# K transposed by crossbar DMA in nearly all heads, and K loads issued in two parts: a two-block attention backward pass

## The chip, the cores and the metric

The kernel runs on one core of a Trainium2 chip. The metric is the device time of one execution in microseconds; three runs of the kernel before gave 1694.41, 1717.56 and 1721.23 us, so the median is 1717.56 us. A core has five engines that run beside each other: PE (TensorE: matrix products and transposes), DVE (VectorE), ACT (ScalarE), POOL (GpSimd) and SP (SyncE, which here only issues DMA transfers). The DMA engines, 16 for this core, move the data. All wait for each other through semaphores.

## The reference

Two independent attention blocks, A and B, with inputs of the same shapes. The kernel computes the output of both and the gradients of all ten inputs.

```python
B, Sq, D = 8, 96, 640
H, Sk, Dh = 32, 512, 128
q = (x @ wq).reshape(B, Sq, H, Dh).transpose(0, 2, 1, 3)
scores = jnp.einsum("bhqd,bhkd->bhqk", q, k_cache) * (Dh ** -0.5)
p = _softmax(scores, axis=-1)
o = jnp.einsum("bhqk,bhkd->bhqd", p, v_cache)
return o.transpose(0, 2, 1, 3).reshape(B, Sq, H * Dh) @ wo
...
_out, _vjp = jax.vjp(_f, A_x, A_k_cache, A_v_cache, A_wq, A_wo, B_x, B_k_cache, B_v_cache, B_wq, B_wo)
_grads = _vjp(grad_out)
```

All tensors are bf16. The K and V caches and their gradients are the large ones: 32 heads x 8 batches x 512 x 128 for each block.

## The kernel before, in words

The unit of work is one (head, batch): 2 blocks x 32 heads x 8 batches = 512 of them, called ticks, at about 3.3 us each. One tick goes through a software pipeline of steps that are spread over later ticks:

- S1 (`c_s1`, L280): K of this batch, 128 x 4 x 128, is transposed in four pieces on PE, and DVE copies the result from PSUM to the tile `KT_pe`. Only for batches that `k_on_pe` (L548) names.
- S2 (`c_s2a`, L291, and `c_s2b`, L304): scores = Q K^T, one matmul of 512 columns (L298) that needs the transposed K; DVE takes the row maximum, ACT the exponential.
- S3 (L315, L324): the reciprocal on DVE, the scaling of P on POOL.
- S4, S5 (`c_s45`, `c_s4`): P transposed on PE, output and dV.
- S6 (`c_s6`, L411): dP, which needs V transposed (`VT`), and dS.
- S7, S8: dK, dS transposed, dQ.

Work of a whole head (projections, transposes of Q and dO, weight gradients) is hooked onto certain ticks of the head, so some ticks hold little more than the pipeline and others twice as much.

**K and V.** `c_ld` (L262) loads the K or V of two batches (a pair, `NB = 2`) with one DMA of 256 KB: 128 partitions, 2 x 512 elements in each. K has 7 buffers, V 5. `c_xt` (L272) transposes a whole pair by a crossbar DMA from SBUF to SBUF: `VT` for all pairs, with 4 buffers, and `KT` for those pairs that are not on PE, with 2 buffers. `k_on_pe` sends to PE every even pair, all pairs of head 0 and, in the first block, those of head 1. That makes 268 batches on PE and 122 pairs (244 batches) by DMA.

**Order.** All loads and crossbar transposes are issued by SP, in one stream in program order; stores of dK and dV and the loads of weights are issued by POOL. The Emitter sorts the steps by tick and by slot within a tick. `OFF` (L45) gives the ticks: the K load of a pair at -5, the V load at -3, KT at -3, VT at 0, S2 at +3, S6 at +6, S8 at +8. S2 and S3 are put in with high priority, and a scheduler may place an instruction later than its tick where a buffer is not yet free. A new KT needs its buffer back: the last reader of the KT of two uses earlier is the second S2 of that pair. The semaphores of SP's DMAs are eight in number and are used in turn.

Of the kernel before, what the change touches and what calls it, by code (L numbers as in the profile page):

```python
# [46 lines left out]
EV = dict(pB0="act", pB1="dve", pC00="act", pC01="act", pC10="act", pC11="dve", pD0="dve", pD1="dve", qA0="act", qA1="dve", qB0="act", qB1="dve", qD="dve", gU="act")  # L47
GSPREAD0 = 9
PRIO_OFF = 2000
GSPREAD1 = 9  # L50
SLOTS = dict(LOAD=0, S2A=5, S2B=5.5, S1=6, S8=10, S7=20, S5=30, S4=40, S6=50, S3A=52, S3B=53, S5B=54, HEAD=SL_HEAD, GRP=SL_GRP)


def build_block(tc, em, tick0, blk, x, kc, vc, wq, wo, g_all, out_all, dx, dk, dv, dwq, dwo, ident, ones, pools, HG=6, first=True, groups=None):
    nc = tc.nc
# [7 lines left out]
    KC = Sk // 128  # L63
    NB = 2
# [197 lines left out]
    def c_ld(h, b, n, bufs):  # L262
        def f():
            src = kc if n == "K" else vc
            X = kvp.tile([128, NB, KC, 128], BF16, name=n + "_sb", bufs=bufs)
            nc.sync.dma_start(X[:], src[b:b + NB, h].rearrange("b (p c) d -> p b c d", c=KC))
            for i in range(NB):
                st = CS.setdefault((blk, h, b + i), {})
                st[n + "_sb"], st[n + "_all"] = X[:, i], X
        return f  # L270
# [20 lines left out]
    def c_s2a(h, b):  # L291
        def f():
            with tc.high_priority(PRIO_OFF):
                st = CS[(blk, h, b)]
                hs = HS[(blk, h)]
                tok = slice(b * Sq, (b + 1) * Sq)
                S_ps = bank([Sq, Sk], F32, "S_ps")
                nc.tensor.matmul(S_ps[:], hs["QT_h"][:, tok], st["KT"], start=True, stop=True)  # L298
                negm = wk.tile([Sq, 1], F32, name="negm", bufs=3)
                nc.vector.tensor_reduce(negm[:], S_ps[:], axis=AX.X, op=ALU.max, negate=True)  # L300
                st["S_ps"], st["negm"] = S_ps, negm
        return f

    def c_s2b(h, b):  # L304
        def f():
            with tc.high_priority(PRIO_OFF):
                st = CS[(blk, h, b)]
                E_sb = wk.tile([Sq, Sk], BF16, name="E_sb", bufs=2)
                rowsum = wk.tile([Sq, 1], F32, name="rowsum", bufs=3)
                nc.scalar.activation(E_sb[:], st["S_ps"][:], ACT.Exp, bias=st["negm"][:], scale=1.0, accum_out=rowsum[:])  # L310
                st["E_sb"], st["rowsum"] = E_sb, rowsum
                del st["S_ps"]
        return f

    def c_s3a(h, b):  # L315
        def f():
            with tc.high_priority(PRIO_OFF):
                st = CS[(blk, h, b)]
                rinv = wk.tile([Sq, 1], F32, name="rinv", bufs=3)
                nc.vector.reciprocal(rinv[:], st["rowsum"][:])  # L320
                st["rinv"] = rinv
        return f

    def c_s3b(h, b):  # L324
        def f():
            with tc.high_priority(PRIO_OFF):
                st = CS[(blk, h, b)]
                P_sb = wk.tile([Sq, Sk], BF16, name="P_sb", bufs=5)
                pinned(nc.gpsimd.tensor_scalar(P_sb[:], st["E_sb"][:], st["rinv"][:], 0.0, op0=ALU.mult, op1=ALU.add))  # L329
                st["P_sb"] = P_sb  # L330
# [215 lines left out]
    NTS = len(tsplits)  # L546

    def k_on_pe(h, b):  # L548
        return (b // NB) % 2 == 0 or h == 0 or (first and h == 1)

    SX = pools["SX"]
    for g in range(NG):
        h0 = GH0[g]
        for hh in range(groups[g]):
            h = h0 + hh
# [16 lines left out]
            for b in range(B):  # L572
                ct = c0t + b
                if b % NB == 0:
                    em.add(tick0 - 12 if first and h == 0 and b == 0 else ct + OFF["ldk"], SLOTS["LOAD"], c_ld(h, b, "K", 7))
                    em.add(ct + OFF["ldv"], SLOTS["LOAD"], c_ld(h, b, "V", 5))
                    if not k_on_pe(h, b):
                        em.add(ct + OFF["kt"], SLOTS["LOAD"] + 1, c_xt(h, b, "KT", 2))
                    em.add(ct + OFF["vt"], SLOTS["LOAD"] + 1, c_xt(h, b, "VT", 4))
                if k_on_pe(h, b):  # L580
                    em.add(ct + 2, SLOTS["S1"], c_s1(h, b))
                em.add(ct + OFF["s2"], SLOTS["S2A"], c_s2a(h, b))
                em.add(ct + OFF["s2"], SLOTS["S2B"], c_s2b(h, b))
                em.add(ct + OFF["s3"], SLOTS["S3A"], c_s3a(h, b))
                em.add(ct + OFF["s3"], SLOTS["S3B"], c_s3b(h, b))
                em.add(ct + OFF["s5"], SLOTS["S5B"], c_s5b(h, b))
                if b % 2 == 1:
                    em.add(ct + OFF["s4"] + 1, 54.3, c_st(h, b, "v"))
                    em.add(ct + OFF["s7"] + 1, 54.3, c_st(h, b, "k"))
                em.add(ct + OFF["s4"], SLOTS["S4"], c_s4(h, b))  # L590
                for i, o in enumerate(("s8", "s7", "s5", "s4")):
                    SX.setdefault(ct + OFF[o], [None] * 4)[i] = (blk, h, b)
                em.add(ct + OFF["s6"], SLOTS["S6"], c_s6(h, b))
                em.add(ct + OFF["s7"], SLOTS["S7"], c_s7(h, b))
# [9 lines left out]
        gs0 = max(3, (GSPREAD0 * groups[g]) // HG)  # L604
        gs1 = max(3, (GSPREAD1 * groups[g]) // HG)
        if not first and g == NG - 2:
# [16 lines left out]
def _kernel_impl(tc, A_x, A_k_cache, A_v_cache, A_wq, A_wo, B_x, B_k_cache, B_v_cache, B_wq, B_wo, grad_out,  # L623
           out_0, out_1, out_2, out_3, out_4, out_5, out_6, out_7, out_8, out_9, out_10, HG=6, slots=None, off=None, hk=None, ev=None, gspread=None, groupsA=None, groupsB=(6, 6, 6, 6, 6, 2)):
    global GSPREAD0, GSPREAD1
    nc = tc.nc
# [8 lines left out]
    if gspread:  # L635
        GSPREAD0, GSPREAD1 = gspread
    with ExitStack() as ctx:
# [104 lines left out]
```

## Time and profile before

| what | before |
|---|---|
| runs | 1694.41, 1717.56, 1721.23 us |
| profiled execution | span 1699.8 us (the page gives no other time of it) |
| granted PE clock | 0.998 |
| PE busy | 1675.7 us (99%) |
| K transposes on PE (L285) | x1072 matmuls, 104.0 us busy |
| copies to KT_pe on DVE (L287) | x268, 410 ns median |
| KT by DMA (L275) | x122, 1250 ns median issue on SP |
| VT by DMA (L275) | x256, 1440 ns median issue on SP |
| K loads (L266) | x256, 256 KB, 5.2 us median to landing |
| mean DMA rate | 249 GB/s |

"Busy" is the time in which an engine, or a group of instructions, has at least one in work. Matmuls are pipelined, so that their durations overlap. A line such as `PE S_ps L298 <- DMA KT<-K_sb: 2.1, 1, 2.1` in the view of waits says that PE stood idle ahead of the instruction that writes S_ps at line 298 until the DMA that writes KT had landed: 2.1 us in total, 1 time, 2.1 us at the longest. PEld is the part of PE that loads the stationary operand, and SPq the sequencer of SP. In a timeline, the columns are start, duration, engine, line, operation and tiles. The share of a DMA queue is the sum of its packets' times over 16 engines; packets of different queues overlap, so that the sum can pass 100%.

### The profile page before, as it was taken

The page shows a single profiled execution, that of the slowest core. Times are in us where ns is not written, and L with a number is a line of the kernel's source. Part 1 is how long each engine was busy: PE and PEld are TensorE (multiplying, and loading weights), DVE is VectorE, ACT ScalarE, POOL GpSimd, SP SyncE. Part 2 cuts the span into 40 slices and gives each one's busy share as a digit, 9 for nine tenths or more (in the row PEclk, how much of TensorE's full clock was granted, in tenths as well). Part 3 has the DMA queues.
Part 4 walks back from the last instruction along what each step waited for, and adds up shares of the span by engine and source line. Part 5 has one row for each costly group of instructions (what it writes and reads, how often), then busy time and mean ns, then how long its engine had stood idle before and what let it go on. Part 6 is the DMA issues. An engine that isn't in the chain of part 4 may idle for free.

```text
span 1699.8 us, 56567 instructions
## 1 busy us (share of the span) xinstructions
PE 1675.7 (99%) x22024; PEld 1343.8 (79%) x22024; DVE 1329.8 (78%) x3052; ACT 1405.2 (83%) x3518; POOL 1040.3 (61%) x1747
## 2 busy tenths in 40 slices
PE   8999999999999999999999999999999999999999
PEld 7877778778778778777778877887788778778876
DVE  6887678878788878787778876787788778878877
ACT  6998889869869869878768998897799679878975
POOL 3676567646647647656566764675576557656754
PEclk9999999999999999999999999999999999999999
DMA  9999999999999999999999999999899989999994
GB/s 256 252 259 250 258 225 260 262 242 243 262 221 252 268 238 259 225 251 237 281 256 269 273 270 248 238 289 248 218 261 276 237 221 261 281 217 240 263 247 141
DMA packets 600429, 423.05 MB, mean 249 GB/s; under 512 B 419360, under 2 KB 557984, under 8 KB 600160
## 3 DMA queue, kind: packets, MB, share of 16 engines
q1 hardware_dynamic: 546576, 242.08, 72.2%
q0 software_dynamic: 53584, 177.35, 32.7%
q8 instruction: 173, 2.83, 0.7%
q14 instruction: 96, 0.79, 0.2%
HBM read 161.09 MB, written 159.12 MB: 188 GB/s over the span
## 4 chain that ended last, share of the span: by engine, by line
PE 89%; DMA 4%; ACT 3%; issue 1%; DVE 1%; POOL 0%; SPq 0%; DVEq 0%; ACTq 0%; POOLq 0%
PE q_ps L243 12%; PE o_ps L512 12%; PE dwo_ps L470 6%; PE dV_ps L389 6%; PE dK_ps L432 6%; PE S_ps L298 6%; PE dP_ps L417 6%; PE dwq_ps L490 6%; PE x_ps L340 5%; PE x_ps L365 5%; PE dst_ps L346 5%; PE x_ps L359 5%; PE kT_ps L285 3%; PE n_ps L258 3%; PE nat_ps L455 2%; DMA VT<-V_sb 1%
## 5 line engine op out<-in xcount | busy, mean ns | idle before, releaser
L329 POOL TENSOR_SCALAR P_sb<-E_sb,rinv 96x512 bf16<-96x512 bf16 x512 | 352.6, 689 | 567.8 <-DVE rinv L320 559.2
L310 ACT ACTIVATE E_sb<-S_ps,negm 96x512 bf16<-96x512 f32 x512 | 351.0, 686 | 187.6 <-DVE negm L300 181.9
L421 DVE SCALAR_TENSOR_TENSOR dS_sb<-dP_ps,dl_ps,P_sb 96x512 bf16<-96x512 f32 x512 | 382.1, 746 | 60.9 <-PE dl_ps L419 54.6
L300 DVE TENSOR_REDUCE negm<-S_ps 96x1 f32<-96x512 f32 x512 | 347.6, 679 | 50.9 <-PE S_ps L298 46.6
L435 ACT ACTIVATE dK_sb<-dK_ps 128x512 bf16<-128x512 f32 x512 | 302.1, 590 | 63.4 <-PE dK_ps L432 56.5
L392 ACT ACTIVATE dV_sb<-dV_ps 128x512 bf16<-128x512 f32 x512 | 311.6, 609 | 0.0
L378 ACT ACTIVATE PT_sb<-x_ps 128x384 bf16<-128x384 bf16 x512 | 253.1, 494 | 0.0
L512 PEld LDWEIGHTS <-OD 128*128 128x128 bf16 x1536 | 132.2, 98 | 100.4 <-issue 1.0
L398 POOL DMA_DIRECT2D out_dram<-dV_sb x256 | 194.9, 761 | 11.8 <-issue 8.6
L398 POOL DMA_DIRECT2D out_dram<-dK_sb x256 | 195.0, 762 | 9.1 <-issue 4.4
L389 PE MATMUL dV_ps<-dOnat_h,P_sb 96*128 96x128 bf16 x2048 | 198.2, 219 | 0.8 <-DVE dOnat_h L160 0.6
L417 PE MATMUL dP_ps<-VT,dOT_h 128*96 128x512 bf16 x512 | 195.4, 382 | 3.0 <-DMA VT<-V_sb 3.0
L432 PE MATMUL dK_ps<-Qnat_h,dS_sb 96*128 96x128 bf16 x2048 | 198.1, 219 | 0.1
L407 POOL TENSOR_TENSOR prod<-OD,dOT_h 128x96 bf16<-128x96 bf16 x512 | 184.2, 360 | 13.8 <-ACT OD L375 12.6
L348 DVE COPY dST_sb<-dst_ps 128x384 bf16<-128x384 bf16 x512 | 177.1, 346 | 10.5 <-PE dst_ps L346 10.3
L365 PE MATMUL x_ps<-ident,P_sb 96*128 96x96 bf16 x2048 | 172.0, 205 | 0.8 <-POOL P_sb L329 0.3
L359 PE MATMUL x_ps<-PT_sb,V_sb 128*128 128x96 bf16 x2048 | 172.3, 206 | 0.2 <-ACT PT_sb L378 0.2
L346 PE MATMUL dst_ps<-ident,dS_sb 96*128 96x96 bf16 x2048 | 172.3, 206 | 0.2 <-DVE dS_sb L421 0.2
L340 PE MATMUL x_ps<-dST_sb,K_sb 128*128 128x96 bf16 x2048 | 171.0, 206 | 1.3 <-ACT dK_sb L435 0.8
L375 ACT ACTIVATE OD<-x_ps 128x192 bf16<-128x192 f32 (+1 forms) x515 | 167.9, 326 | 3.9 <-PE x_ps L340 3.9
L320 DVE RECIPROCAL rinv<-rowsum 96x1 f32<-96x1 f32 x512 | 79.9, 156 | 106.0 <-ACT E_sb L310 100.4
L340 PEld LDWEIGHTS <-K_sb 128*128 128x128 bf16 x2048 | 131.1, 98 | 25.1 <-issue 1.6
(84 smaller groups left out, 3744.4 us busy)
## 6 DMA issues: line engine op xcount, KB each, us to landing
out_dram<-dV_sb POOLq DMA_DIRECT2D x256, 256.0 KB, 5.2
out_dram<-dK_sb POOLq DMA_DIRECT2D x256, 256.0 KB, 5.3
K_sb<-in_A_k_cache_dram SPq DMA_DIRECT2D x128, 256.0 KB, 5.3
V_sb<-in_A_v_cache_dram SPq DMA_DIRECT2D x128, 256.0 KB, 5.2
K_sb<-in_B_k_cache_dram SPq DMA_DIRECT2D x128, 256.0 KB, 5.0
V_sb<-in_B_v_cache_dram SPq DMA_DIRECT2D x128, 256.0 KB, 4.9
out_dram<-dwo_sb POOLq DMA_DIRECT2D x63, 160.0 KB, 4.8
out_dram<-dwq_sb POOLq DMA_DIRECT2D x31, 320.0 KB, 6.1
```

The source lines that it names most:

```text
L300: nc.vector.tensor_reduce(negm[:], S_ps[:], axis=AX.X, op=ALU.max, negate=True)
L310: nc.scalar.activation(E_sb[:], st["S_ps"][:], ACT.Exp, bias=st["negm"][:], scale=1.0, accum_out=rowsum[:])
L329: pinned(nc.gpsimd.tensor_scalar(P_sb[:], st["E_sb"][:], st["rinv"][:], 0.0, op0=ALU.mult, op1=ALU.add))
L340: nc.tensor.matmul(dQT_ps, st["K_sb"][:, c, :], st["dST_sb"][:, c * Sq:(c + 1) * Sq], start=(c == 0), stop=(c == KC - 1))
L389: nc.tensor.matmul(dV_ps[:, c * 128:(c + 1) * 128], P_sb[:, c * 128:(c + 1) * 128], hs["dOnat_h"][:, b * 128:(b + 1) * 128], start=True, s ...
L392: nc.scalar.activation(SB[(blk, h, b // 2, "v")][:, b % 2], dV_ps[:], ACT.Identity, scale=1.0)
L398: pinned(nc.gpsimd.dma_start(dst[b - 1:b + 1, h].rearrange("b (p c) d -> p b (c d)", c=KC), SB.pop((blk, h, b // 2, which))[:]))
L417: nc.tensor.matmul(dP_ps[:], hs["dOT_h"][:, tok], st["VT"], start=True, stop=True)
L421: nc.vector.scalar_tensor_tensor(dS_sb[:], dP_ps[:], dl_ps[:, 0:1], st["P_sb"][:], op0=ALU.subtract, op1=ALU.mult)
L432: nc.tensor.matmul(dK_ps[:, c * 128:(c + 1) * 128], dS_sb[:, c * 128:(c + 1) * 128], hs["Qnat_h"][:, b * 128:(b + 1) * 128], start=True, s ...
L435: nc.scalar.activation(SB[(blk, h, b // 2, "k")][:, b % 2], dK_ps[:], ACT.Identity, scale=1.0)
L512: nc.tensor.matmul(o_ps[:], src[:, t * 128:(t + 1) * 128], rhs, start=(hh == 0), stop=(hh == groups[g] - 1))
```

## The change

K of every head but the first (in the first block: but the first two) is transposed by crossbar DMA; and each K load becomes two DMAs on SP, one for partitions 0 to 119 and one for 120 to 127. The data and the arithmetic stay the same. `KT` keeps its 2 buffers, and `OFF` is unchanged.

```diff
+SPLIT_LD = ("K",)
...
             X = kvp.tile([128, NB, KC, 128], BF16, name=n + "_sb", bufs=bufs)
-            nc.sync.dma_start(X[:], src[b:b + NB, h].rearrange("b (p c) d -> p b c d", c=KC))
+            v = src[b:b + NB, h].rearrange("b (p c) d -> p b c d", c=KC)
+            if n in SPLIT_LD:
+                nc.sync.dma_start(X[0:120], v[0:120])
+                nc.sync.dma_start(X[120:128], v[120:128])
+            else:
+                nc.sync.dma_start(X[:], v)
...
     def k_on_pe(h, b):
-        return (b // NB) % 2 == 0 or h == 0 or (first and h == 1)
+        return h == 0 or (first and h == 1)
```

After it, 24 batches are left on PE (8 of head 0 in each block, 8 of head 1 in the first), and 244 pairs go by DMA in place of 122. SP issues 512 K load DMAs in place of 256.

## The prediction

> **What bounds the kernel now.** I read the page from the top: busy shares, the chain that ended last, the DMA queues; then the waits, the tile views of the two crossbar-transposed tiles, and a timeline of one tick.
>
> ```profile
> PE 1675.7 (99%) x22024; PEld 1343.8 (79%) x22024; DVE 1329.8 (78%) x3052; ACT 1405.2 (83%) x3518; POOL 1040.3 (61%) x1747
> ...
> q1 hardware_dynamic: 546576, 242.08, 72.2%
> q0 software_dynamic: 53584, 177.35, 32.7%
> ...
> PE 89%; DMA 4%; ACT 3%; issue 1%; DVE 1%; POOL 0%; SPq 0%; DVEq 0%; ACTq 0%; POOLq 0%
> ```
>
> TensorE (PE) is never idle and holds 89% of the chain; nothing else is near. But the two DMA queues add up to 105% of 16 engines: the transfers are the second limit, and close. They are hidden today, as the waits show:
>
> ```profile
> PE dP_ps L417 <- DMA VT<-V_sb: 3.0, 2, 2.4
> ...
> PEld L298 <- DMA KT<-K_sb: 2.5, 2, 2.3
> ...
> PE S_ps L298 <- DMA KT<-K_sb: 2.1, 1, 2.1
> ```
>
> PE stood still for transposed tiles for under 8 us in the whole run. How long they take from issue to landing (min/median/max, first KT, then VT):
>
> ```profile
> L275 SPq DMA_TRANSPOSE KT<-K_sb x122: 1231/1250/3126, 44.3 to 1647.3; - x122
> ...
> DMA to landing us min/median/max: 3.1/5.2/11.9
> ```
>
> ```profile
> L275 SPq DMA_TRANSPOSE VT<-V_sb x256: 1231/1440/6143, 12.2 to 1656.9; - x128
> ...
> DMA to landing us min/median/max: 3.1/6.1/14.9
> ```
>
> And what four K transposes cost on PE, from one tick:
>
> ```profile
> 807.75 0.39 PE L285 MATMUL kT_ps<-ident,K_sb 128*128 128x128 bf16 x4
> 807.92 0.24 PEld L340 LDWEIGHTS <-K_sb 128*128 128x128 bf16 x4
> 807.97 0.33 PE L340 MATMUL x_ps<-dST_sb,K_sb 128*128 128x96 bf16 x4
> ```
>
> The next group starts 0.22 us after this one: 0.22 us is the price, not the 0.39 us of the row. The 1072 such matmuls end 56 ns apart in the median.
>
> **The change part by part.**
>
> *Removed from PE.* 268 of 512 batches are transposed on PE now; afterwards 24 are (8 of head 0 in each block, 8 of head 1 in the first). 244 x 4 x 56 ns = 55 us, with the slower first ones 56 us. PE is the bound, so this counts in full: 1699.8 - 56 = 1644 us. Row against rule: in this row a matmul lasts 219 ns but ends 56 ns after the last. The Trainium skill, page "Trainium Kernel Development and Optimization", section Performance Expectations, warns that matmul busy time is a bad metric because matmuls are pipelined; agreed. By the busy time of the group (104.0 us for 1072) the gain would be 95 us.
>
> *Removed from DVE.* 244 copies KT_pe x 410 ns = 100 us, off a 78% busy engine. Nothing on the path: PE waited 0.8 us for them. ACT stays at 1405 us, 85% of 1644, and does not become the bound.
>
> *Added to SP and the DMA engines.* 122 KT transposes (122 x 1.40 us mean issue = 171 us of SP) and 256 more load issues (about 0.48 us each, the K_sb load's median: 123 us). SP's loads and transposes take 939 us today, so 1233 of 1644 us afterwards, in order. Per pair (two ticks, 6.4 us) that is five DMAs. Each waits for the one eight places before it, 10 us earlier, where 95% of the VT have landed (10.2 us): a rare wait. V and K loads keep leads of 24 and 35 us, VT one of 18 to 20 us, against landings of 5 to 6: costed at nothing, and only a landing over 15 us would uncover them.
>
> *The wait that is added.* KT has two buffers. Today only odd pairs use them, so a KT is issued some 20 us before its S2. Afterwards every pair does: KT of pair p may be issued only when PE has done the second S2 of pair p-2, three ticks before its own S2. In the built order of the changed kernel this wait stands on every KT. I counted the PE instructions from that release to the first S2 of the pair, each at the pace at which such matmuls end in this trace (56 ns for 128 columns, 43 for 96, about 216 for 512), scaled by 1.036 to the span: 7.0 us in the shortest twentieth, 8.6 median, 10.9 upper quartile (a tick without head work is short). SP takes about 0.4 us of it on average, finishing the VT issued just before. Behind the waiting KT on SP stand the next V and K loads, whose leads bear it; behind the waiting S2 on PE stands all of PE, so a late KT costs its full lateness.
>
> How late? Pairing every such lead with every landing time of today's 122 KT: 5% are late, 0.063 us on average, x 244 = 15 us. With those of the 256 VT: 19%, 0.34 us, x 244 = 82 us. These are my bounds. Today's KT is issued a median 4.2 us behind its VT, afterwards 1.3 us, so it will queue behind it. The nearest rows lie between: 39 transposes issued 2.0 to 2.6 us behind another landed in 6.3 us median, ten under 2.0 us behind in 5.3. I take the middle, 48 us, less 8 us for the split (next): 40 us.
>
> *The split.* In the packet records of this trace the transposes (256-byte packets, 18 ns in the median) freeze 235 times on nearly all engines at once, for 0.96 us in the median, 230 us in all, and all end together; inside, about one packet of that queue is in progress: one engine catches up, and the others stand. In 59% of these an instruction fetch began in the 2 us before (28% at random moments). An engine that moves no K would be spared 256 x 16 packets x 42 ns = 174 us. The skill, "DMA: Bandwidth & Descriptors", section Why a DMA increments its semaphore by 16 and not by 1, says that the engine count is the largest number up to 16 dividing the outer dimension, on the lowest-numbered engines: 15 for 120 partitions, 8 for 8, so the last engine carries no K. The same page's Rules for kernel authors speak against it: two transfers to disjoint partitions are not worth it, one of 128 partitions is better. No row shows either. By the first rule, if the last engine is the laggard, landings shorten: VT's landings cut by a tenth make 47 us of the 82, KT's make 8 of the 15. By the second the split gives nothing. From the rows alone: bounds 0 (another engine lags) and 35 us (that tenth of VT's landings); I take 8, near the lower end, since no row names the laggard.
>
> *Sum.* -56 + 40 = -16 us on 1699.8, i.e. 1684. The page gives the span alone; the three runs are 1694 to 1721, and the median 1717.6 lies 17.8 above the span, which I keep: 1701.6.
>
> **The rivals.**
>
> *The waits stay small.* If the split removes most freezes, landings fall by a tenth (8 us of waits, from KT): -48, 1669 us. For: PE waits under 8 us for transposes now. Against: the lead shrinks from 20 to 8.6 us.
>
> *Slower: KT waits take more than PE gave.* One mechanism: VT and KT back to back on SP, KT landing like VT or later. VT's landings give -56 + 82 = +26, 1744 us; a tenth longer 131 us of waits, +75, 1792 us. For: 32% more transposes on queues already at 105%. Against: a waiting PE lets the DMA drain, and one late KT gives the next more time. It decides from 0.23 us mean wait per KT (no gain), 0.37 us for 2% slower.
>
> *The hardware queue becomes the bound.* q1 has a packet in flight for 1382 us; 122 transposes more, 2.36 us from first to last packet each, make 1670 us, plus the 24 us in which PE idles today: 1694 span, 1712 us. Against: 0.6 us of the 2.36 are freezes, and packets of two transfers overlap.
>
> *The split does nothing:* the forecast without its 8 us, 1709 us; within its range.
>
> **How the numbers follow.** Forecast 0.40 (its own range 1677 to 1744, waits of 15 to 82 us); small waits 0.25; slower 0.27; queue bound 0.08. A measurement here tells about 2% from no change: 1683 and 1752. Faster: 0.25 plus 0.08 of the forecast's low end = 0.33. Slower: 0.25 of the 0.27. Within: 0.42. The range reaches from 1660 (no waits: 1662) to 1785; about 0.06 lie below and 0.12 above.
>
> **What would show it** (line numbers of the changed kernel, six or seven higher). K transposes on PE, L291, x96, and copies KT_pe x24; PE's work shorter by 56 us; waits of PE and PEld at S2, L304, for KT, 15 to 82 us in all; KT landing near 6 us; SP waiting at L281 for S2. Wrong if those waits pass 110 us, if PE waits for VT or V_sb, or if KT waits stay under 10 us and the span is near 1650. The split's step is right if freezes and VT's landing shrink.

## The result and the profile after

| | before | after |
|---|---|---|
| median | 1709.61 us (1694.41 to 1721.23, 4 runs) | 1873.73 us (1855.3 to 1881.82, 4 runs) |
| ratio, 95% interval | | 1.0973 [1.0882, 1.1065] |
| span of the profiled execution | 1699.8 us | 1853.5 us |
| granted PE clock, mean | 0.998 | 0.969 |
| PE idle (worked out from the PE records) | 19 us | 170 us |

The changed kernel is 9.7% slower, and its time lies above the range that was given. (The profiled execution of before took 1701.65 us: its span lies 1.85 us under its own time, so the 17.8 us between span and median that the prediction kept are mostly the spread between executions.)

The page of after: busy shares, the two DMA queues, and the chain that ended last, by engine and by line.

```profile
PE 1677.7 (91%) x21048; PEld 1318.8 (71%) x21048; DVE 1258.3 (68%) x2808; ACT 1407.5 (76%) x3518; POOL 1039.4 (56%) x1747
...
q1 hardware_dynamic: 677200, 274.08, 79.5%
q0 software_dynamic: 53584, 177.35, 30.3%
...
PE 58%; DMA 36%; ACT 3%; issue 1%; DVE 1%; POOL 0%; SPq 0%; DVEq 0%; ACTq 0%; POOLq 0%
DMA KT<-K_sb 35%; PE o_ps L518 11%; PE q_ps L244 6%; PE dwq_ps L496 5%; PE S_ps L304 4%; PE dwo_ps L476 4%; PE dK_ps L438 4%; PE dV_ps L395 4%; PE dP_ps L423 4%; PE dst_ps L352 3%; PE x_ps L371 3%; PE x_ps L346 3%; PE x_ps L365 3%; PE n_ps L259 2%; PE nat_ps L461 1%
```

976 matmuls went (22024 to 21048: 244 x 4), yet PE's busy time did not fall. PE held 89% of the chain before; now it holds 58%, and one transfer, K's transpose, 35%. The view of waits names the same transfer:

```profile
PEld L304 <- DMA KT<-K_sb: 170.1, 93, 5.6
PE S_ps L304 <- DMA KT<-K_sb: 148.6, 82, 5.4
```

Both lines are one stall seen by PE's two halves. No line of this view names VT, V_sb or a K load for PE. Issue times on SP in the tile views of KT and of VT (min/median/max in ns):

```profile
L281 SPq DMA_TRANSPOSE KT<-K_sb x244: 1232/2775/5037, 40.2 to 1811.7; - x122
```

```profile
L281 SPq DMA_TRANSPOSE VT<-V_sb x256: 1231/1392/5444, 14.1 to 1810.3; - x128
```

The median issue of a KT went from 1250 to 2775 ns; that of a VT stayed. The last three columns of the view by windows are granted clock, DMA share and GB/s. First two windows of before, then the same two of after and a short one:

```profile
300.00:600.00 300.00, 299.33 (x3927) 238.91 (x3925) 240.81 (x554) 247.30 (x621) 184.79 (x310) 1.00 1.08 250
900.00:1200.00 300.00, 299.68 (x3996) 241.68 (x3994) 232.82 (x531) 263.20 (x661) 193.09 (x324) 1.00 1.09 260
```

```profile
300.00:600.00 300.00, 274.14 (x3500) 215.11 (x3500) 211.78 (x473) 231.42 (x581) 173.32 (x292) 0.99 1.15 251
900.00:1200.00 300.00, 275.83 (x3442) 216.05 (x3440) 201.76 (x452) 232.22 (x583) 175.01 (x293) 0.96 1.10 253
...
990.00:995.00 5.00, 3.93 (x26) 2.59 (x27) 1.75 (x4) 1.26 (x3) 0.39 (x1) 0.50 1.39 310
```

The DMA engines move as many GB/s as before (251 and 253 against 250 and 260) while there is more to move; the share was 1.08 to 1.09 before and is 1.10 to 1.15 now. One stall: first the last reader of the KT two uses earlier, in the view of L304 for 973 to 978 us, then the timeline of after.

```profile
L304 PE MATMUL S_ps<-KT,QT_h x1: 379/379/379, 975.3 to 975.3; 128*96 128x512 bf16 x1
```

```profile
975.89 0.33 SPq L270 DMA_DIRECT2D K_sb<-in_B_k_cache_dram  x1
976.32 5.44 SPq L281 DMA_TRANSPOSE VT<-V_sb  x1
981.87 3.76 SPq L281 DMA_TRANSPOSE KT<-K_sb  x1
...
984.00 0.34 PE L365 MATMUL x_ps<-PT_sb,V_sb 128*128 128x96 bf16 x4
...
991.07 0.63 PE L304 MATMUL S_ps<-KT,QT_h 128*96 128x512 bf16 x1 [4.82 <-DMA KT<-K_sb]
...
994.26 0.53 PE L365 MATMUL x_ps<-PT_sb,V_sb 128*128 128x96 bf16 x4
```

PE freed the KT buffer at 975.7 us (975.3 and 0.38). SP had the second part of a K load and a VT to issue first, and the VT took it 5.44 us; the KT came only then, 6.2 us after its release, and landed 9.1 us later. PE stood still for 4.8 us. From 989.0 us, still within the stall, its clock is granted at one half for 6.8 us (0.50 in the short window): the same four matmuls of L365 take 0.53 us in place of 0.34.

**The account.** 1699.8 - 56 (K transposes off PE) + 151 (PE idle, 19 to 170 us) + 53 = 1848 us, against a span of 1853.5. The 56 us are the prediction's estimate, by the count of matmuls. The 53 us: within the span the clock was granted at 0.5 in 27 stretches of 3.4 or 6.8 us, 112.6 us in all, which loses 56.3 us; before, two such stretches lost 3.4 us. In the records each of the 27 begins inside a gap in PE's work of 1.8 to 6.5 us or within 8 us after it; ten gaps of that size were followed by none. That explains why PE's busy time did not fall.

### The profile page after: what moved, and what is told of

Same layout as the page of the kernel before. It is cut to its first block, busy times and chain, and to the rows that moved or that the text cites. A ratio compares the mean times of both kernels' runs of the same rounds, so it can differ in the third digit from the quotient of the medians.

```text
span 1853.5 us, 55160 instructions
## 1 busy us (share of the span) xinstructions
PE 1677.7 (91%) x21048; PEld 1318.8 (71%) x21048; DVE 1258.3 (68%) x2808; ACT 1407.5 (76%) x3518; POOL 1039.4 (56%) x1747
## 3 DMA queue, kind: packets, MB, share of 16 engines
HBM read 161.09 MB, written 159.12 MB: 173 GB/s over the span
## 4 chain that ended last, share of the span: by engine, by line
PE 58%; DMA 36%; ACT 3%; issue 1%; DVE 1%; POOL 0%; SPq 0%; DVEq 0%; ACTq 0%; POOLq 0%
DMA KT<-K_sb 35%; PE o_ps L518 11%; PE q_ps L244 6%; PE dwq_ps L496 5%; PE S_ps L304 4%; PE dwo_ps L476 4%; PE dK_ps L438 4%; PE dV_ps L395 4%; PE dP_ps L423 4%; PE dst_ps L352 3%; PE x_ps L371 3%; PE x_ps L346 3%; PE x_ps L365 3%; PE n_ps L259 2%; PE nat_ps L461 1%
## 5 line engine op out<-in xcount | busy, mean ns | idle before, releaser
L304 PE MATMUL S_ps<-KT,QT_h 128*96 128x512 bf16 x488 | 193.9, 397 | 152.7 <-DMA KT<-K_sb 148.6
L395 PE MATMUL dV_ps<-dOnat_h,P_sb 96*128 96x128 bf16 x2048 | 203.0, 223 | 0.6 <-DVE dOnat_h L161 0.6
L438 PE MATMUL dK_ps<-Qnat_h,dS_sb 96*128 96x128 bf16 x2048 | 203.3, 223 | 0.0
L423 PE MATMUL dP_ps<-VT,dOT_h 128*96 128x512 bf16 x512 | 199.6, 390 | 0.2
L304 PEld LDWEIGHTS <-QT_h 128*96 128x96 bf16 x512 | 63.3, 124 | 189.1 <-DMA KT<-K_sb 170.1
L371 PE MATMUL x_ps<-ident,P_sb 96*128 96x96 bf16 x2048 | 175.9, 208 | 1.3 <-POOL P_sb L335 0.8
L352 PE MATMUL dst_ps<-ident,dS_sb 96*128 96x96 bf16 x2048 | 176.2, 209 | 1.0 <-DVE dS_sb L427 0.2
L365 PE MATMUL x_ps<-PT_sb,V_sb 128*128 128x96 bf16 x2048 | 176.5, 209 | 0.2 <-ACT PT_sb L384 0.2
L346 PE MATMUL x_ps<-dST_sb,K_sb 128*128 128x96 bf16 x2048 | 175.6, 210 | 0.0
```

The costliest lines, as they stand in the source:

```text
L395: nc.tensor.matmul(dV_ps[:, c * 128:(c + 1) * 128], P_sb[:, c * 128:(c + 1) * 128], hs["dOnat_h"][:, b * 128:(b + 1) * 128], start=True, s ...
L423: nc.tensor.matmul(dP_ps[:], hs["dOT_h"][:, tok], st["VT"], start=True, stop=True)
L438: nc.tensor.matmul(dK_ps[:, c * 128:(c + 1) * 128], dS_sb[:, c * 128:(c + 1) * 128], hs["Qnat_h"][:, b * 128:(b + 1) * 128], start=True, s ...
```

## The experiments

Five theories were named for the loss. A: KT is late for want of lead, so that a third buffer mends it. B: the 16 DMA engines are the bound; any work added there costs time, whoever reads it. C: the split of the loads is what costs. D: SP's stream of issues, in order, is the bound. S: SP stands waiting for a K load that has just been issued, and everything behind it is late. A was my first theory.

The table gives all runs. Ratios are against the kernel before on the same chip. "Packets" is the time of all packets of q0 and q1 per engine (their shares x span); "SP" is the time that all DMA issues of SP take; "KT wait" is the wait of PE (S_ps) for KT. The last three columns are those of the profiled execution, whose span is given; it can lie above the median (e2: 1849 against 1828).

| run | median us | ratio [95%] | span us | packets us | SP us | KT wait us |
|---|---|---|---|---|---|---|
| before | 1709.61 | 1 | 1699.8 | 1783 | 963 | 2 |
| after | 1873.73 | 1.0973 [1.0882, 1.1065] | 1853.5 | 2036 | 1479 | 149 |
| e1_split_only | 1736.84 | 1.0162 [1.0042, 1.0281] | 1742.2 | 1908 | 1084 | 19 |
| e2_dma_only | 1828.46 | 1.0683 [1.058, 1.0786] | 1849.4 | 1986 | 1412 | 144 |
| e3_kt3 | 1841.86 | 1.0776 [1.0692, 1.0859] | 1832.6 | 2079 | 1629 | 131 |
| e4_kt3_nosplit | 1786.84 | 1.0431 [1.0305, 1.0557] | 1797.6 | 1986 | 1514 | 107 |
| e5_dummy_kt | 1863.17 | 1.0903 [1.0817, 1.099] | 1864.6 | 1999 | 1114 | 59 |
| e6_small_stores | 1681.14 | 0.9832 [0.9782, 0.9882] | 1680.1 | 1678 | 1218 | 25 |
| e7_k_load_pool | 2018.99 | 1.1659 [1.1542, 1.1776] | 2002.4 | 2209 | 1688 | 254 |
| e8_five_eighths | 1719.9 | 1.0048 [1.0007, 1.0089] | 1698.3 | 1829 | 1014 | 10 |
| e9_dummy_old_k | 1823.0 | 1.0574 [1.046, 1.0688] | 1827.8 | 2047 | 1571 | 28 |
| e10_quarter | 1713.47 | 1.0035 [0.9973, 1.0097] | 1715.6 | 1641 | 785 | 0 |
| e11_dummy_copy | 1771.84 | 1.0346 [1.026, 1.0432] | 1772.2 | 1931 | 1229 | 21 |
| e12_split64 | 1723.38 | 1.0082 [1.0018, 1.0147] | 1723.7 | 1853 | 1151 | 9 |

**e1: only the split** (after, with the old choice of batches).

```diff
-        return h == 0 or (first and h == 1)
+        return (b // NB) % 2 == 0 or h == 0 or (first and h == 1)
```

> The split load alone: K again half on TensorE as before, each K load as 120 + 8 partitions. Theory A (the added time is KT issued late for want of a third buffer; the split matters little): within 1% of before, 1695 to 1725 us, waits for KT at S2 under 15 us. Theory B (the DMA queues are the bound once all KT are on them): also near before, since the bytes are the same. Theory C (the split is what costs: SP issues 256 more DMAs and the 8-partition part is slow): clearly slower, 1750 us or more.

1.6% slower, with an interval from 0.4 to 2.8%. The freezes of the transposes (in the packet records, eight or more 256-byte packets of over 0.3 us that end together) went from 235, 230 us in all, to 275, 237 us in all, the mean landing of VT from 6.47 to 6.68 us. The 1024-byte packets of the loads of K and V last 57.9 ns on average in place of 52.6, the transposes' packets 33.8 ns in place of 31.3. The split takes no freeze away, and the packets become longer.

**e2: only the DMA transposes** (after, K loads whole).

```diff
-SPLIT_LD = ("K",)
+SPLIT_LD = ()
```

> All KT by DMA, loads not split, two KT buffers. Theory A: nearly as slow as the changed kernel, 1830 to 1880 us; the two issues that SP saves per pair (0.33 us) take some 20 us off the lateness at most; KT waits at S2 stay above 200 us of PE and PEld together. Theory B: as the changed kernel or slower, 1860 to 1920 us, as the last DMA engine gets its K packets back. Theory C: back near 1700 us.

6.8% slower. So the transposes bring most of the 9.7%, and the split some 2.5% on top of them (1873.73 / 1828.46). PE's wait for KT is 144 us without the split and 149 us with it. C falls as the main cause; its cost is real.

**e3 and e4: a third KT buffer**, with the split (e3) and with the K loads whole, `SPLIT_LD = ()` (e4).

```diff
-                        em.add(ct + OFF["kt"], SLOTS["LOAD"] + 1, c_xt(h, b, "KT", 2))
+                        em.add(ct + OFF["kt"], SLOTS["LOAD"] + 1, c_xt(h, b, "KT", 3))
```

> The changed kernel with three KT buffers in place of two, nothing else. The release of a KT buffer then comes five ticks ahead of its use and not three. Theory A: the waits for KT fall under 30 us, the half-clock stretches of TensorE go, and PE's removed work shows: 1660 to 1700 us. Theory B (queues or SP are the bound): SP still issues five DMAs per pair at the same cost and the queues move the same packets, so 1790 us or more stay. Theory C: above 1750 us.

> All KT by DMA with three KT buffers, loads not split. Theory A: 1660 to 1710 us, within 1.5% of the same with the split. Theory B: 1790 us or more, and slower than the same with the split. Theory C: the fastest of these four, about 1660 us, and over 3% faster than the same with the split.

The waits of e3 (those of after: 170.1 and 148.6):

```profile
PEld L304 <- DMA KT<-K_sb: 153.3, 73, 7.4
PE S_ps L304 <- DMA KT<-K_sb: 130.8, 59, 7.2
```

The buffer does what it should: between the release of a KT's buffer and its first S2 lie 16.1 us of PE work in place of 9.5. But SP now issues the KT 7.5 us after the release in place of 1.95, the issue lasts 3.1 us and the landing 7.3. The added lead is eaten ahead of the transfer and in it. It helps by 1.7% (1841.86 against 1873.73) and leaves the kernel slower than before. A, my first theory, falls: the lead grew by 6.6 us, and PE's wait went only from 149 to 131 us. Of the 1817 us by which the KT are issued after their release in e3, 1649 are taken by other issues of SP (VT 641, earlier KT 571, loads 437). So SP's stream, which D names, is where the lead goes; why its issues take so long is for e6 to tell. Without the split 3% come back again (1786.84 / 1841.86).

**e6: less traffic, same transposes** (after; the stores of dK and dV keep their number and write only partitions 0 to 15).

```diff
-            pinned(nc.gpsimd.dma_start(dst[b - 1:b + 1, h].rearrange("b (p c) d -> p b (c d)", c=KC), SB.pop((blk, h, b // 2, which))[:]))
+            pinned(nc.gpsimd.dma_start(dst[b - 1:b + 1, h].rearrange("b (p c) d -> p b (c d)", c=KC)[0:16], SB.pop((blk, h, b // 2, which))[0:16]))
```

> The changed kernel, split loads and two KT buffers, but each store of a dK or dV pair moves 16 of its 128 partitions: seven eighths of these two outputs are left out. Same issues, same waits, less traffic. Theory B: the packets' time falls by 365 us per engine to 1671, over 1.10 that is 1520, so TensorE is the bound again: 1645 to 1700, KT landing in about 5 us. Theory A: KT is released as late as before and its wait stays above 100 us in all, 1760 or more. Theory D: SP still issues five DMAs per pair, 1780 or more.

The queues and the waits of e6:

```profile
q1 hardware_dynamic: 677200, 274.08, 86.5%
q0 software_dynamic: 29008, 59.91, 13.3%
```

```profile
PEld L304 <- DMA KT<-K_sb: 34.2, 31, 2.6
...
PE S_ps L304 <- DMA KT<-K_sb: 25.4, 22, 2.3
```

And the issue of its KT, in the tile view:

```profile
L281 SPq DMA_TRANSPOSE KT<-K_sb x244: 1231/1790/4302, 39.7 to 1634.9; - x122
```

SP's queue carries the same packets as in after; only POOL's queue lost its bytes. KT still has two buffers, with 9.2 us of PE work from release to use. Yet KT waits fall from 149 to 25 us, the mean KT issue from 2.72 to 1.93 us (the medians in the tile views: 2.78 and 1.79), its mean landing from 6.64 to 5.04 us, the loss by half clock from 56 to 7 us, and the kernel is 10% faster than after and 1.7% faster than before, which does the whole output. That is against A, and against D as far as D means the number of issues: neither was changed, and SP's 1305 issues take 1218 us in place of 1479. What was too little in after is room for the transfers. Two limits of this run: the kernel before was not run with small stores, so how much of the 1.7% is PE's gain is not shown; and fewer bytes in stores also mean fewer bytes to HBM (41.68 MB written in place of 159.12) and less work for POOL (941 us busy in place of 1039, though POOL held 0% of after's chain). e9 and e11 below add transfers without either.

**e5: the other 122 transposes in the kernel before, read by nobody.** PE keeps its K transposes.

```diff
+                    elif not (h == 0 or (first and h == 1)):
+                        em.add(ct + OFF["kt"], SLOTS["LOAD"] + 1, c_xt(h, b, "KX", 1))
```

> The kernel before, unsplit, with 122 more crossbar transposes: the K pairs that TensorE transposes are also transposed by DMA into a scratch tile with one buffer that nobody reads. No work of the reference is left out; the added DMAs are waste. Theory B (the DMA engines are the bound: before, their packets take 1783 us per engine, 1.05 of the span; the highest share seen in any run is 1.13): 234 us of packets more make 2017, over 1.10 that is 1834 us, so 1790 to 1860, though no TensorE instruction waits for the scratch tile. Theory A (late KT for want of lead): the KT that are used keep their 20 us of lead, so 1700 to 1740. Theory D (SP's in-order issue stream is the bound): SP issues two loads and two transposes per pair, 5.9 of 6.6 us, so 1700 to 1760.

9% slower, but not by the cause it was made for. The scheduler put each scratch transpose right behind its own K load, so SP stood waiting for fresh loads. SP's waits in e5:

```profile
SPq L275 <- DMA K_sb<-in_B_k_cache_dram: 312.5, 123, 8.0
SPq L275 <- DMA K_sb<-in_A_k_cache_dram: 311.1, 120, 6.0
```

These were 152.0 and 169.4 us before, and the landings are not longer than before (KT 4.76 us on average, 5.24 before). Here S acts. In after, SP's longest wait is for PE, and no row for a load passes 6 us; the first row of that view:

```profile
SPq L281 <- PE S_ps L304: 148.8, 74, 5.4
```

The run does not part B from S, so it was made again without that wait.

**e9: the same, reading K of two pairs earlier**, which landed long ago.

```diff
+    def c_kx(h, b):
+        def f():
+            KX = kvp.tile([128, NB * KC, 128], BF16, name="KX", bufs=1)
+            old = CS[(blk, h, b - 4) if b >= 4 else (blk, h - 1, b + 4)]["K_all"]
+            pinned(nc.sync.dma_start_transpose(KX[:], old[:].rearrange("p a c d -> p (a c d)")))
+        return f
...
+                    elif not (h == 0 or (first and h == 1)):
+                        em.add(ct + OFF["kt"], SLOTS["LOAD"] + 1, c_kx(h, b))
```

> As the run with 122 scratch transposes, but each scratch transpose reads the K of two pairs earlier, which landed long ago, and keeps its place in SP's order: SP does not stand waiting for a fresh K load ahead of it, as it did 623 us in that run (321 before). No work of the reference is left out. Theory B (the DMA engines cannot carry 122 transposes more): the same packets as there, 1780 to 1860 us. Theory S (that run was slow because SP, issuing in order, waited for each K load to land ahead of a transpose): 1700 to 1740 us.

The waits of e9, then its windows:

```profile
PE dP_ps L424 <- DMA VT<-V_sb: 49.4, 21, 6.6
...
PEld L305 <- DMA KT<-K_sb: 34.7, 21, 3.2
...
PE S_ps L305 <- DMA KT<-K_sb: 27.7, 18, 3.0
```

```profile
300.00:600.00 300.00, 279.37 (x3548) 223.09 (x3573) 219.83 (x503) 225.67 (x563) 167.17 (x281) 0.97 1.15 246
900.00:1200.00 300.00, 281.04 (x3602) 225.18 (x3631) 216.22 (x492) 235.74 (x591) 175.87 (x296) 0.97 1.15 251
```

SP's waits for K loads are 23 us in all here. The run is 5.7% slower with transposes that no engine waits for, as B has it and S does not. The loss does not sit at one wait any more, it is spread over VT and the old KT, both of which had long leads (before, 18.5 and 16.1 us on average from issue to first use; VT's mean landing rose from 6.47 to 7.58 us). The windows show the share and the rate at which after stood. By itself the run does not part B from D: SP's issues take 608 us more, of which the scratch transposes are 303; the rest is that the others lengthen, a VT's issue from 1.68 to 2.53 us on average. e6 showed that such issues shorten with the traffic.

**e11: e9 with a plain copy of the same bytes.**

```diff
-            pinned(nc.sync.dma_start_transpose(KX[:], old[:].rearrange("p a c d -> p (a c d)")))
+            pinned(nc.sync.dma_start(KX[:].rearrange("p a k -> p (a k)"), old[:].rearrange("p a c d -> p (a c d)")))
```

> As the run with 122 scratch transposes of old K (1823 us), but each scratch transfer is a plain copy of the same 256 KB from SBUF to SBUF, in the same place of SP's order. No work of the reference is left out. Theory B in its narrow form (what the engines lack is packet time: a transpose is 1024 packets of 256 bytes, about 1.9 us per engine): a plain copy has far fewer packets and, at the rate of the K load (0.8 us per engine), adds 100 us and not 230 to the 1783, over 1.10 that is 1710: 1700 to 1740. If the bytes are what counts: 1790 to 1830, as the transposes. If only the place in SP's order counts: the same 1790 to 1830.

3.5%, between the two expectations. The queues of e11 (before: 72.2% and 32.7% of a span of 1699.8 us):

```profile
q1 hardware_dynamic: 564144, 274.06, 74.8%
q0 software_dynamic: 53584, 177.35, 34.1%
```

A copy has 128 packets of 2048 bytes, 88 ns each on average: 122 of them take 86 us of each engine. A transpose has 1024 packets of 256 bytes, 31 ns each: 242 us for 122. The packets of the others stretch too (the 4096-byte packets of the stores from 204 to 222 ns, in e9 and e11 alike), and all packets together rise by 148 us per engine in e11 and 264 in e9. The span rises by 72 and by 128 us, about in proportion; by the ratios it is some 60 and 98 us. So neither the bytes nor the place in SP's order can be all of it, since these are the same in both runs and the cost is not. That it is engine time that costs, in degrees, fits best; B's narrow form, a hard ceiling, had put e11 at 1700 to 1740 us. How much the place in SP's order adds is not separated. Traffic to HBM is not what was added: its bytes are the same in before, after, e9 and e11 (161.09 MB read, 159.12 MB written).

**e7: K loads issued by POOL in place of SP** (from e4).

```diff
-                nc.sync.dma_start(X[:], v)
+                (nc.gpsimd if n == "K" and not (first and h == 0) else nc.sync).dma_start(X[:], v)
```

> All KT by DMA, three KT buffers, loads not split, and the K loads issued by GpSimd and not by SP (the first head's aside). SP issues three DMAs per pair and not four; the bytes are the same. To be compared with the run of the same name without that move, 1787 us. Theory B: 1760 to 1820, no gain over 1.5%. Theory D: SP's 0.6 us per pair come off the span, 1787 - 256 x 0.6 = 1630, so TensorE's 1645 to 1700.

2019 us, missed by every theory. POOL scales P between S2 and the rest, and now it also stands waiting until a K buffer is free. From the waits of e7:

```profile
POOL K_sb L272 <- PE x_ps L346: 258.2, 41, 11.9
PE S_ps L304 <- DMA KT<-K_sb: 254.4, 64, 10.5
```

It put a new wait on POOL's in-order stream, so it does not test D cleanly. SP's time did not fall: with 252 issues fewer than in e4 it rose from 1514 to 1688 us.

**e8 and e10: other doses**, 5/8 of the pairs by DMA (e8, from e4) and about a quarter (e10, from before).

```diff
+        return (b // NB) % (2 if h % 2 == 0 else 4) == 0 or h == 0 or (first and h == 1)   # e8
...
+        return (b // NB) % 4 != 3 or h == 0 or (first and h == 1)                          # e10
```

> Half of the K pairs by DMA in even heads, three quarters in odd heads, three KT buffers, loads not split: the dose between before and all. Theory B: packets 1783 + 58 = 1841 us per engine, over 1.10 1673, while TensorE's work falls by 14 us to 1686: within 1% of before, 1690 to 1730. Theory A: with three buffers no KT is late, 1685 to 1705. Theory D: as B.

> The kernel before with only the fourth K pair of a head by DMA (61 pairs and not 122), the rest on TensorE. Theory B: TensorE's work grows by 28 us and is the bound, 1700 + 28 + the usual 18 us around: 1725 to 1750. A theory in which the transfers already held up the kernel before would have it no slower, 1690 to 1715.

e8 is no faster than before, though PE lost transposes (and KT has three buffers there). e10 gives PE some 28 us more work (488 matmuls, an estimate at 56 ns each), and I expected 1725 to 1750 us; it took 1713, the same as before within its interval, and no PE instruction waited for KT. So between a quarter and 5/8 the time is flat within about 1%: most of what PE gains there the transfers already give back. The kernel before stood at the crossing, not ahead of it.

**e12: the split in equal halves, alone** (e1 with partitions 0 to 63 and 64 to 127).

```diff
-                nc.sync.dma_start(X[0:120], v[0:120])
-                nc.sync.dma_start(X[120:128], v[120:128])
+                nc.sync.dma_start(X[0:64], v[0:64])
+                nc.sync.dma_start(X[64:128], v[64:128])
```

> The kernel before with each K load issued as partitions 0 to 63 and 64 to 127 in place of 0 to 119 and 120 to 127 (the latter run: 1737 us, ratio 1.016). If the price of the split is SP's second issue and the second fixed latency of a transfer, the same: 1725 to 1750. If it is the uneven spread of 120 and 8 partitions over the engines, it goes: 1700 to 1718.

0.8% against e1's 1.6%; the intervals overlap, so it is not shown how much of e1's cost is the second DMA per load and how much the uneven parts. The load packets last 56.1 ns here, 57.9 ns at 120 and 8, 52.6 ns whole.

## Why the prediction was wrong

**Removed from PE: right.** 976 matmuls are gone from PE's work. In e6, where the transfers have room, PE's busy time is 1615.0 us against 1675.7 before (some 9 us of the difference are 161 matmul records that this trace lacks); in after the half clock hides it.

**Removed from DVE: right in kind.** 244 instructions fewer; its busy time fell by 71.5 us, not by 100; DVE was not on the path, so nothing came of it.

**The wait that is added: here the prediction failed.** Its place was right (L304, for KT), its lead too: 9.5 us of PE work from release to use, on average. KT lands in 6.64 us on average, about where the upper bound had it (VT before: 6.47). What failed is the step "SP takes about 0.4 us of it on average, finishing the VT issued just before": SP took 1.95 us, and over 4.7 us in the last twentieth. Of 471 us of such lateness, 260 went to the issue of a VT and 88 to K loads. Pairing the leads of after with the VT landings of before, as the prediction did, gives 72 us of waits with 0.4 us and 228 us with the measured lateness. Measured were 149 us, where the sum had 40; that one late KT gives the next more time, as the prediction said, fits the difference from 228.

**Added to SP** was counted from the issue times of before: loads and transposes 1233 us; measured 1461 us. The 244 KT alone took 664 us, 2.72 us each, in place of the 1.40 us counted. An issue's time is not fixed: the same 244 took 1.93 us each in e6, with fewer bytes in the other queue. What an issue waits for in that time the trace does not show.

**Under both lies one omission: the DMA engines' room.** The text says that the queues add up to 105% and that the transfers are "the second limit, and close", and then prices no step by it. The sum was in the rows: packets 1783 us per engine, plus 122 x 1024 x 31.3 ns / 16 = 244 us, make 2027 us (measured 2036). Divided by the share that the windows of before show in steady work, 1.09, this is 1860 us of span; 1853.5 came. So close a fit is partly luck: the sum leaves out the split, which alone added 125 us of packet time in e1, and the transposes' packets came out shorter (29.3 ns in e2, whose packets make 1986 us). The rival "the hardware queue becomes the bound" had the mechanism nearly right and got 1694 us, because it added up only the times in which q1 has a packet in flight; e6 shows that q0's bytes slow q1's transfers too. The rival "KT waits take more than PE gave" was nearest, with 1744 to 1792 us; what was said against it (a waiting PE lets the DMA drain, a late KT gives the next more time) was too weak.

**Not in the sum at all: the clock.** 53 us went to the half-clock stretches around stalls. With the 109 us by which the waits for KT passed the 40 of the sum, this makes 162 of the some 169 us between the predicted span, 1684 us, and the measured one.

**The split: wrong in sign.** It was costed at -8 us between 0 and -35; alone it costs 1.6%, with the transposes 2.5 to 3%. The freezes stayed (289, 244 us in all, in after), so sparing an engine the K packets does not end them. That the split does use fewer engines fits the packet counts: q1 has 1792 packets more in e1 than before, 7 for each load, as 15 and 8 end packets in place of 16 make. The time so spared was put at 42 ns a packet, 174 us; the 1024-byte packets of before last 52.6 ns on average, but no term of the sum rests on it. The rule of the Trainium skill that the prediction quoted against the split ("DMA: Bandwidth & Descriptors", Rules for kernel authors: two transfers to disjoint partition halves are not worth it) is about halves, as in e12; there these runs agree: 64 and 64 gained nothing and cost 0.8%.

**Still open.** How packets of the two queues lengthen each other, why an issue on SP lengthens with the traffic, and which engine is the last in a freeze: the trace does not tell the engines apart. A shift of the VT issue to another place in SP's stream was not tried. No version with the whole output was faster than the kernel before.

## What to carry to other kernels

Before work is moved to DMA, add up the packet time of all queues, add that of the new transfers from the rows of the same kind, and divide by the highest share that a window of steady work shows: if this exceeds the span of the bounding engine, expect the transfers to become the bound, however well they seem hidden. Here this is a rough guide and no law: with 1.09 it gives 1860 us for after and for e9 (spans 1853.5 and 1827.8), and 1715 us for e11, whose span was 1772.2. Before, PE waited under 8 us for transposed tiles at a share of 1.05, and e8 and e9 found no room left: small waits say nothing about room. A third buffer buys lead only where the transfer can start: see first when its queue comes to it (in e3, 7.5 us after the release).

## What was not expected of the hardware

- A DMA transpose of 256 KB takes 2.0 us of each engine (1024 packets x 31.3 ns / 16), a plain copy of the same bytes 0.70 us (128 x 88 ns / 16): 2.8 times. The Trainium skill, "Advanced Engine Details and Errata", section X-Bar Transpose (TRN2), says that transpose DMAs are as fast as regular ones; for these SBUF-to-SBUF transfers, in this mix, the measurement decides otherwise.
- The issue of a KT on SP is no fixed price: 1.25 us in the median before (3.1 at most), 2.78 us in after (5.0 at most), 1.79 us in e6.
- During or after a stall the PE clock was granted at 0.5 for 3.4 or 6.8 us; 27 such stretches in after cost 56 us. The Trainium skill, "TensorE: Matmul & The Clock Gate", Part 1, describes this: half rate after an idle window of about 3.4 us, full rate after a busy one. The trace agrees with the lengths. It does not agree on the idle time: 16 of the 27 had no gap in PE's work over 3.4 us ahead of them, and 1.8 us was enough for the shortest.
- Splitting the K loads in two lengthened the 1024-byte packets, K's and V's taken together (52.6 to 57.9 ns in e1), without a byte more; in e6, with little traffic of stores, they still last 57.3 ns.
